# A spectral block and a GeGLU block on one core: last filter groups in other banks, squares a slice later, two norms on Pool, the table load behind the first x pieces

## The chip, the cores and the metric

The kernel runs on one core of a Trainium2 chip. The metric is the device time of one execution in microseconds (us). The kernel before takes 511.15 us (median of 4 runs, 511.12 to 511.28). A profile is one execution recorded by the hardware; its span is about 2 us shorter than the device time (509.6 us for the profiled run of the kernel before, which took 511.58 us), as the device time contains what surrounds the span.

Engines: PE multiplies matrices, DVE (VectorE), ACT (ScalarE) and Pool (GpSimd) do the elementwise work, SP here only issues transfers. The program gives each engine its own list of instructions, in an order stated by hand, and makes it wait on semaphores for the others. Matmuls write their results to PSUM, of which the program uses eight banks, numbered 0 to 7, and DVE or ACT evict them (copy them out) to SBUF. Idle matmuls are matmuls whose results are never used.

## The reference

```python
def reference(A_x, A_w_r, A_w_i, B_x, B_w_gate, B_w_up, B_w_down):   # x: 1 x 2048 x 576 bf16
    x = A_x
    # irfft2(rfft2(layernorm(x)) * (w_r + i w_i)), over the 2048 and the 576
    h = x + _A_ref(_layernorm(x, axis=-1), A_w_r, A_w_i)
    # (gelu(n @ w_gate) * (n @ w_up)) @ w_down, hidden size 4608
    return h + _B_ref(_layernorm(h, axis=-1), B_w_gate, B_w_up, B_w_down)
```

The first half is a two-dimensional Fourier filter, computed with matmuls against cosine tables. The second half is a gated feed-forward block, about 427 of the 510 us.

## The kernel before

The program runs through five stages.

1. Start, up to about 22 us. x arrives in five pieces (rows of tiles 0-1, 2-3, 4-7, 8-11, 12-15). Mean and variance of each 128-row tile come from DVE (`bn_stats`) or, for tiles 3, 7, 11 and 13, from ACT. A table ATB is scaled by each tile's reciprocal deviation (ATS), PE multiplies, ACT and DVE evict to U.
2. The d transform, 22 to 53 us: sixteen filter groups, each through D (PE, sums on DVE into CUS), B (PE, evicted by ACT into YS), products with the filter (T1, T2 on DVE), their difference and sum (ZS, on Pool), and V (PE, evicted by ACT).
3. The tail: the last three groups' V.
4. The inverse: sixteen slices, `st_I` then `st_N`, residual added on DVE. The first four tiles are also normed and transposed on PE here for the next stage.
5. Gate/up and down products, from 82.5 us to the end.

The parts that matter, with cuts marked by `...`:

```python
# start: loads
for i, (c0, c1) in enumerate(((0, 2), (2, 4), (4, 8), (8, 12), (12, 16))):
    P.dma(SP, XO[:, c0:c1, 0:D], xv[:, c0:c1, :], f"x{i}", ...)
P.dma(ACT, ATB[...], dram["ATAB"][:, :], "atb", w=["ATB"])        # 512 KB
...
# start: order of the statistics (each call adds instructions to one or two engines)
ln1_act(3); idle_mm(18); ln1_tile(0); ln1_tile(1); ln1_var(0); ln1_sqrt(0)
ln1_act(7); ln1_tile(2); ln1_scale(0, POOL); ln1_var(1); ln1_sqrt(1); ...
ln1_sqrt(3); ln1_tile(12); ln1_scale(3, POOL); ln1_var(4); ...

# d transform, group i (st_B, its last lines): Pool but for the last two groups
ze = POOL if i < NG - 2 else DVE
P.op(ze, ... ZS[:, z3, 0, 0:KW] = T1[..., 0, :] - T1[..., 1, :] ...)
P.op(ze, ... ZS[:, z3, 1, 0:KW] = T2[..., 0, :] + T2[..., 1, :] ...)

def st_V(i):                                    # all groups in banks 6 and 7
    for c in range(3):
        for zp in range(2): P.op(PE, ... matmul(bank(6 + c // 2, ...), ZS[...], VT[...]) ...)
    P.op(ACT, ... V[:, :, :, g, :] <- banks 6, 7 ...)

for i in range(NG + 3):                         # NG = 16
    if i < NG: st_D(i)
    if 1 <= i <= NG: st_B(i - 1)
    if i > NG: idle_ft(5, 2 * (i - NG - 1))     # idle matmuls
    if i >= 3: st_V(i - 3)
idle_ft(5, 4)

# inverse
def st_N(c):
    ... four matmuls ...; DVE: x[c] += result, with its row sum
    if c < 4: square(c, ...)                    # ACT: row sum of squares of x[c]
TURN = (7, 9, 11, 13)                           # slices after which a tile is transposed
for c in range(NT):
    if c == 6: ln2_b(0)                         # ACT: sqrt
    st_I(c)                                     # 6 matmuls, ACT evicts into GS
    if c >= 1: st_N(c - 1)
    if c == 5: ln2_a(0)                         # DVE: three small ops
    if c == 6: ln2_c(0)                         # DVE: reciprocal
    if c in (6, 8, 10, 12): norm((c - 6) // 2)  # DVE
    if c in TURN: turn_pe(TURN.index(c))        # PE transpose, ACT evicts
```

Of the kernel before, what the change touches and what calls it, by code (L numbers as in the profile page):

```python
# [4 lines left out]
BF16 = mybir.dt.bfloat16  # L5
F32 = mybir.dt.float32
ACTF = mybir.ActivationFunctionType
ALU = mybir.AluOpType

S, D, K2 = 2048, 576, 289  # L10
# [5 lines left out]
NG = 16  # L16
# [279 lines left out]
def _build(nc, A_x, A_w_r, A_w_i, B_w_gate, B_w_up, B_w_down, out):  # L296
    P = Prog(nc)
# [6 lines left out]
    sb = SbufMap(nc, base, top)  # L304
    XO = sb.alloc("XO", [128, NT, D], BF16)
    WGU = sb.alloc("WGU", [128, 9, FF], BF16)
    HN = sb.alloc("HN", [128, 2, 640], BF16)
    IDT = sb.alloc("IDT", [128, 128], BF16)
    ST1 = sb.alloc("ST1", [128, NT, 2, 6], F32)
    MV1 = sb.alloc("MV1", [128, NT, 2], F32)  # L310
# [40 lines left out]
    T1 = sb.alloc("T1", [128, 2, 2, KW], BF16)  # L351
    T2 = sb.alloc("T2", [128, 2, 2, KW], BF16)
    ZS = sb.alloc("ZS", [128, 3, 2, ZW], BF16)
    SQ = sb.alloc("SQ", [128, 2, D], BF16)
    sb.off = v_off
    AT = sb.alloc("AT", [128, 36, 512], BF16)
    HT1 = sb.alloc("HT1", [128, 5, 512], BF16)
# [16 lines left out]
    ov = out[0].rearrange("(p c) d -> p c d", c=NT)  # L374
    for i, (c0, c1) in enumerate(((0, 2), (2, 4), (4, 8), (8, 12), (12, 16))):
        P.dma(SP, XO[:, c0:c1, 0:D], xv[:, c0:c1, :], f"x{i}", w=[("X", c) for c in range(c0, c1)])
    P.dma(ACT, ATB[:, :, :].rearrange("p a b -> p (a b)"), dram["ATAB"][:, :], "atb", w=["ATB"])
    P.dma(SP, FT[:, :, :, :].rearrange("p a b c -> p (a b c)"), dram["FTAB"][:, :], "ft", w=["FT"])
    P.dma(SP, BT[:, :, :, :].rearrange("p a b c -> p (a b c)"), dram["BTAB"][:, :], "bt", w=["BT"])
    P.dma(SP, VT[:, :, :, :].rearrange("p a b c -> p (a b c)"), dram["VTAB"][:, :], "vt", w=["VT"])  # L380
# [57 lines left out]
    def ln1_scale(i, eng):  # L438
        c0, c1 = GROUPS[i]
        P.op(DVE, lambda v, c0=c0, c1=c1: v.reciprocal(RS1[:, c0:c1], RS1[:, c0:c1]), r=[("SD1", i)], w=[("RS1", i)])  # L440
        if eng == POOL:
            P.op(POOL, lambda g, c0=c0, c1=c1: g.tensor_tensor(ATS[:, c0:c1, :], ATB[:, c0:c1, :],
                                                               RS1[:, c0:c1].unsqueeze(2).to_broadcast([128, c1 - c0, 128]), op=ALU.mult),
                 r=[("RS1", i), "ATB"], w=[("ATS", c) for c in range(c0, c1)])
        else:
            for c in range(c0, c1):
                P.op(DVE, lambda v, c=c: v.tensor_scalar(ATS[:, c, :], ATB[:, c, :], RS1[:, c:c + 1], None, op0=ALU.mult),
                     r=[("RS1", i), "ATB"], w=[("ATS", c)])
# [43 lines left out]
    ln1_sqrt(0)  # L492
    ln1_act(7)
    ln1_tile(2)
    ln1_scale(0, POOL)
    ln1_var(1)
    ln1_sqrt(1)
    ln1_tile(4)
# [14 lines left out]
    ln1_var(3)  # L513
    ln1_sqrt(3)
    ln1_tile(12)
    ln1_scale(3, POOL)
    ln1_var(4)
    idle_mm(5)
    a_group(2, A5, lambda: ln1_sqrt(4), 2)
    ln1_tile(14)  # L520
# [30 lines left out]
    def st_B(i):  # L551
        g = GORD[i]
        sl = i % 2
        sp_ = 1 if g == 0 else 0

        for b, tabs in ((4, (0, 1, 3)), (5, (1, 2, 0))):
            for m, (tb, pl, q0, q1) in enumerate(((tabs[0], 0, 0, K2), (tabs[1], 1, 0, HK), (tabs[2], 1, HK, K2))):
                P.op(PE, lambda t, b=b, tb=tb, pl=pl, q0=q0, q1=q1, m=m, sl=sl, sp_=sp_: t.matmul(  # L558
                    bank(b, 0, 128, q0, q1), BT[:, sp_, tb, :], CUS[:, sl, pl, q0:q1], start=(m == 0), stop=(m == 2)),
                    r=[("CU", sl), ("SU", sl), "BT"], w=[("PS", b)])  # L560
        P.op(ACT, lambda a, sl=sl: a.activation(YS[:, sl, :, 0:K2], banks(4, 2, K2), ACTF.Copy), r=[("PS", 4), ("PS", 5)], w=[("Y", sl)])  # L561
        wk = wkeys[0 if 1 <= g < 9 else 1] + ["Wz", "Yz", "Zz"]
        P.op(DVE, lambda v, g=g, sl=sl: v.tensor_tensor(T1[:, sl, :, :], YS[:, sl, :, :], WS[:, g, :, :], op=ALU.mult), r=[("Y", sl)] + wk, w=[("T1", sl)])
        P.op(DVE, lambda v, g=g, sl=sl: v.tensor_tensor(T2[:, sl, :, :], YS[:, sl, :, :], WS[:, g, 1::-1, :], op=ALU.mult), r=[("Y", sl)] + wk, w=[("T2", sl)])  # L564
        z3 = i % 3
        ze = POOL if i < NG - 2 else DVE
        P.op(ze, lambda v, sl=sl, z3=z3: v.tensor_tensor(ZS[:, z3, 0, 0:KW], T1[:, sl, 0, :], T1[:, sl, 1, :], op=ALU.subtract), r=[("T1", sl)], w=[("Z", z3, 0)])
        P.op(ze, lambda v, sl=sl, z3=z3: v.tensor_tensor(ZS[:, z3, 1, 0:KW], T2[:, sl, 0, :], T2[:, sl, 1, :], op=ALU.add), r=[("T2", sl)], w=[("Z", z3, 1)])  # L568

    def st_V(i):  # L570
        g = GORD[i]
        sl = i % 3
        sp_ = 1 if g == 0 else 0
        for c in range(3):
            b, o = 6 + c // 2, 256 * (c % 2)
            for zp in range(2):
                P.op(PE, lambda t, b=b, o=o, c=c, zp=zp, sl=sl, sp_=sp_: t.matmul(bank(b, 0, 128, o, o + 256), ZS[:, sl, zp, 128 * c:128 * c + 128],  # L577
                                                                                  VT[:, sp_, zp, :], start=(zp == 0), stop=(zp == 1)),
                     r=[("Z", sl, 0), ("Z", sl, 1), "Zz", "VT"], w=[("PS", b)])
        P.op(ACT, lambda a, g=g: a.activation(V[:, :, :, g, :], PS[:, 6 * 512:6 * 512 + 768].rearrange("p (k n e) -> p k n e", k=6, n=16), ACTF.Copy),  # L580
             r=[("PS", 6), ("PS", 7), "Vfree"], w=[("V", g)])

    def idle_ft(n, b):
        for _ in range(n):
# [4 lines left out]
    for i in range(NG + 3):  # L589
        if i < NG:  # L590
            st_D(i)
        if 1 <= i <= NG:
            st_B(i - 1)
        if i > NG:
            idle_ft(5, 2 * (i - NG - 1))
        if i >= 3:
            st_V(i - 3)
    idle_ft(5, 4)


    wdv = B_w_down[:, :].rearrange("(c p) d -> p c d", p=128)
# [8 lines left out]
    P.alias(["FT", "BT", "VT"], [("HT", 0, i, k) for i in range(4) for k in range(5)])  # L610


    vkeys = [("V", g) for g in range(NG)]


    TURN = (7, 9, 11, 13)

    def islot(c):
        return (c + sum(c > t for t in TURN)) % 2
# [16 lines left out]
    def st_N(c):  # L636
        sl = c % 2
        for h in range(2):
            b = 4 + 2 * sl + h
            for i in range(2):  # L640
                rhs = GS[:, sl, i, 288:0:-1] if h else GS[:, sl, i, 0:288]
                P.op(PE, lambda t, b=b, h=h, i=i, c=c, rhs=rhs: t.matmul(bank(b, 0, 128, 0, 288), IT[:, h * i, c, :], rhs, start=(i == 0), stop=(i == 1)),  # L642
                     r=[("G", sl), "IT"], w=[("PS", b)])
        x2 = XO[:, c, 0:D].rearrange("p (a b) -> p a b", a=2)
        P.op(DVE, lambda v, x2=x2, c=c, sl=sl: v.scalar_tensor_tensor(x2, banks(4 + 2 * sl, 2, 288), 1.0, x2, op0=ALU.mult, op1=ALU.add,  # L645
                                                               accum_out=SB2[:, 0, c:c + 1]),
             r=[("PS", 4 + 2 * sl), ("PS", 5 + 2 * sl)], w=[("X", c), ("S0", c)])
        if c < 4:
            square(c, SQ[:, sl, :], ("SQ", sl))


    def ln2_a(q):
# [11 lines left out]
        c0, c1 = ((0, 4), (4, 16))[q]  # L664
        P.op(DVE, lambda v, c0=c0, c1=c1: v.reciprocal(RS2[:, c0:c1], RS2[:, c0:c1]), r=[("SD2", q)], w=[("RS2", q)])

    def norm(c):
        hs = c % 2
        q = min(c // 4, 1)
        for i, (o0, o1, x0, x1) in enumerate(((0, D, 0, D), (D, 640, 512, D))):  # L670
            P.op(DVE, lambda v, c=c, hs=hs, o0=o0, o1=o1, x0=x0, x1=x1: v.tensor_scalar(HN[:, hs, o0:o1], XO[:, c, x0:x1], TM[:, 1, c:c + 1],
                                                                                        RS2[:, c:c + 1], op0=ALU.subtract, op1=ALU.mult),
                 r=[("X", c), ("MN", q), ("RS2", q)], w=[("HN", hs, i)])

    def turn_dma(c):
        hs = c % 2
        q = c // 4
        HT = HTS[q % 2]
        for k in range(5):
            P.dma(SP, HT[:, k, 128 * (c % 4):128 * (c % 4) + 128], HN[:, hs, 128 * k:128 * k + 128], f"tr{c}",  # L680
                  r=[("HN", hs, 0), ("HN", hs, 1)], w=[("HT", q % 2, c % 4, k)], transpose=True)

    def turn_pe(c):
        hs = c % 2
        t0, t1 = 128 * c, 128 * c + 128
        b0 = 2 * ((TURN[c] + 1 + c) % 2)
        for k in range(5):
            b, o = b0 + k // 4, 128 * (k % 4)
            P.op(PE, lambda t, b=b, o=o, k=k, hs=hs: t.matmul(bank(b, 0, 128, o, o + 128), HN[:, hs, 128 * k:128 * k + 128], IDT[:, :], start=True, stop=True),  # L689
                 r=[("HN", hs, 0), ("HN", hs, 1), "IDT"], w=[("PS", b)])  # L690
        P.op(ACT, lambda a, t0=t0, t1=t1, b0=b0: a.activation(HT0[:, 0:5, t0:t1], PS[:, b0 * 512:b0 * 512 + 640].rearrange("p (k e) -> p k e", k=5), ACTF.Copy),
             r=[("PS", b0), ("PS", b0 + 1)], w=[("HT", 0, c, 0)])

    for c in range(NT):
        if c == 6:
            ln2_b(0)
        st_I(c)
        if c >= 1:
            st_N(c - 1)
        if c == 5:  # L700
            ln2_a(0)
        if c == 6:
            ln2_c(0)
        if c in (6, 8, 10, 12):
            norm((c - 6) // 2)
        if c in TURN:
            turn_pe(TURN.index(c))


    fdead = vkeys + ["DT", "IT", ("G", 0), ("G", 1), ("Y", 0), ("Y", 1), "Yz", "Zz", ("SQ", 0), ("SQ", 1)]  # L710
    fdead += [(n_, a) for n_ in ("T1", "T2", "E") for a in range(2)] + [("Z", a, b_) for a in range(3) for b_ in range(2)]
    fnew = ([("AT", f) for f in range(36)] + [("GL", 0), ("GL", 1)] + [("HT", 1, i, k) for i in range(4) for k in range(5)])

# [100 lines left out]
```

## Time and profile before

The head of the page of the kernel before, with the span and the busy time of each engine (share of the span, number of instructions):

```profile
span 509.6 us, 10004 instructions
...
PE 497.7 (98%) x4337; PEld 289.6 (57%) x4337; DVE 183.1 (36%) x375; ACT 158.6 (31%) x296; POOL 42.1 (8%) x60
```

PE is busy nearly always, but this counts idle matmuls too, so it doesn't tell what a change of the first 82 us is worth. The chain of waits does: it goes back from the last instruction to whatever released each step. Its columns are the start, the duration and the work.

```profile
1.67 6.46 DMA XO<-in_A_x_dram
...
85.17 70.04 PE PS L731 x648
155.21 35.39 PE PS L752 x288
```

From 85 us on the chain is PE alone, in four pairs of stretches of 70.0 and 35.4 us. Ahead of that the chain goes through many engines, and it begins with a wait for x. Only this first part can be shortened by the change. It is best cut at four moments, which I read from the timeline:

| kernel before | us |
|---|---|
| ACT begins tile 7, the first use of x piece 2 | 8.15 |
| first D matmul | 22.05 |
| first matmul of the inverse | 59.16 |
| first gate/up matmul | 82.46 |
| end of the span | 509.6 |

In the timeline the columns are start, duration, engine, line of the program, operation, output and inputs, count, and in brackets how long the engine idled before it and what released it. A count, with its duration, stops where the window asked for ends, so the same group can show x12 in one view and x5 in another. `SPq` and `ACTq` are issues of transfers. The start, before:

```profile
0.74 0.37 ACTq L206 DMA_DIRECT2D ATB<-c_atab  x1
...
0.75 2.57 SPq L206 DMA_DIRECT2D XO<-in_A_x_dram  x5
...
6.17 0.68 ACT L411 ACTIVATE JNK<-XO 128x576 bf16<-128x576 bf16 x1 [3.53 <-DMA XO<-in_A_x_dram]
...
8.15 0.68 ACT L411 ACTIVATE JNK<-XO 128x576 bf16<-128x576 bf16 x1 [0.36 <-DMA XO<-in_A_x_dram]
...
15.85 0.98 DVE L430 SCALAR_TENSOR_TENSOR MV_54<-SA,TM 128x1 f32<-128x1 f32 x1
...
22.05 1.66 PE L541 MATMUL PS<-FT,U 128*128 128x290 bf16 x12 [0.35 <-DVE U L474]
```

The table and the five pieces of x are issued at the same moment, on two queues. ACT waits for x piece 2 until 8.15 us. One 128x1 statistics op on DVE (line 430) takes 0.98 us; the same line takes 0.16 us elsewhere in this trace.

The tail of the d transform, before:

```profile
51.82 0.82 POOL L567 TENSOR_TENSOR ZS<-T_80 128x290 bf16<-128x290 bf16 x1 [0.40 <-DVE T_80 L563]
...
52.79 0.96 POOL L568 TENSOR_TENSOR ZS<-T_81 128x290 bf16<-128x290 bf16 x1
...
53.89 0.81 PE L577 MATMUL PS<-VT,ZS 128*128 128x256 bf16 x6 [0.22 <-POOL ZS L568]
...
55.61 0.83 PE L577 MATMUL PS<-VT,ZS 128*128 128x256 bf16 x6 [0.28 <-ACT V L580]
...
56.48 0.81 ACT L580 ACTIVATE V<-PS 128x768 bf16<-128x768 f32 x1 [0.92 <-PE PS L577]
...
57.34 0.83 PE L577 MATMUL PS<-VT,ZS 128*128 128x256 bf16 x6 [0.28 <-ACT V L580]
...
59.16 1.66 PE L627 MATMUL PS<-DT,V 128*128 128x289 bf16 x12 [0.37 <-ACT V L580]
```

Two Pool ops make group 13's ZS. Then V of groups 13, 14 and 15 and their evictions alternate, since they share banks 6 and 7, and the inverse starts behind the last eviction.

A piece of the inverse, before:

```profile
62.40 0.68 ACT L633 ACTIVATE SQ<-XO 128x576 bf16<-128x576 bf16 x1 [0.89 <-DVE XO L645]
...
63.08 0.63 ACT L629 ACTIVATE GS<-PS 128x578 bf16<-128x578 f32 x1
...
63.77 0.67 PE L642 MATMUL PS<-GS,IT 128*128 128x288 bf16 x4 [0.22 <-ACT GS L629]
...
69.59 0.67 PE L642 MATMUL PS<-GS,IT 128*128 128x288 bf16 x4 [0.29 <-ACT GS L629]
```

On ACT a square waits for DVE's new x, the next eviction (GS) queues behind the square, and PE waits for that eviction: at 63.77, at 66.65 in the same way, and at 69.59 (there behind the sqrt).

### The profile page before, as it was taken

Reading aid. Unit: us, or ns where it says so; the run is one execution under the profiler, and the core shown is the slowest. Engines: PE = TensorE matmul, PEld = TensorE weight load, DVE = VectorE, ACT = ScalarE, POOL = GpSimd, SP = SyncE. Lnnn points to the kernel's source line nnn. Section 1 sums busy time; section 2 is a strip of 40 time slices with the busy share of each in tenths; the row PEclk is TensorE's granted clock in tenths of the full one; section 3 lists DMA queues with packets and bytes.
Section 4 is the critical chain, followed back from the end, with each engine's and each line's share of the span. In section 5 each row is a group of like instructions: output and inputs, shape, how many; then the busy total and the mean of one; then the engine's idle time right before and its main releaser. Section 6 shows DMA issues by size and latency. Waiting matters only on the chain.

```text
span 509.6 us, 10004 instructions
## 1 busy us (share of the span) xinstructions
PE 497.7 (98%) x4337; PEld 289.6 (57%) x4337; DVE 183.1 (36%) x375; ACT 158.6 (31%) x296; POOL 42.1 (8%) x60
## 2 busy tenths in 40 slices
PE   6899899999999999999999999999999999999997
PEld 2578565444447774444467754444577644444776
DVE  5899464334431113433321124333311133333111
ACT  6778676664230003232310022333200132323000
POOL 3278910000000000000000000000000000000000
PEclk9999999999999999999999999999999999999999
DMA  8679798000100000110000001100000000000000
GB/s 320 134 259 309 224 343 277 1 1 17 27 12 9 16 19 17 23 22 1 1 7 18 13 15 24 23 7 1 1 17 19 13 1 1 1 1 1 13 18 19
DMA packets 25660, 28.64 MB, mean 56 GB/s; under 512 B 11408, under 2 KB 19600, under 8 KB 25488
## 3 DMA queue, kind: packets, MB, share of 16 engines
q1 hardware_dynamic: 22896, 16.86, 11.4%
q0 software_dynamic: 2576, 10.62, 6.2%
q8 instruction: 34, 0.56, 0.5%
q10 hardware_dynamic: 144, 0.52, 0.3%
q14 instruction: 10, 0.08, 0.1%
HBM read 23.66 MB, written 2.36 MB: 51 GB/s over the span
## 4 chain that ended last, share of the span: by engine, by line
PE 90%; DVE 4%; ACT 3%; DMA 1%; POOL 1%; issue 1%; SPq 0%; DVEq 0%; POOLq 0%
PE PS L731 55%; PE PS L752 28%; PE PS L577 2%; PE PS L541 2%; DMA XO<-in_A_x_dram 1%; PE PS L642 1%; PE PS L558 1%; PE PS L627 1%; DVE XO L645 1%; DVE U L474 1%; ACT U L476 1%; ACT V L580 0%; ACT JNK L411 0%; POOL ZS L568 0%; PE PS L689 0%
## 5 line engine op out<-in xcount | busy, mean ns | idle before, releaser
L743 ACT ACTIVATE GL<-PS 128x512 bf16<-128x512 f32 x144 | 85.9, 597 | 289.9 <-PE PS L731 289.9
L744 DVE TENSOR_TENSOR AT<-GL,PS 128x512 bf16<-128x512 bf16 x144 | 98.9, 688 | 174.2 <-PE PS L731 172.5
L731 PE MATMUL PS<-HT_69,WGU 64*128 64x512 bf16 x1296 | 144.4, 376 | 0.0
L731 PE MATMUL PS<-HT_85,WGU 64*128 64x512 bf16 x1296 | 144.4, 376 | 0.0
L752 PE MATMUL PS<-WD,AT 128*128 128x288 bf16 x1152 | 141.8, 286 | 0.0
L752 PEld LDWEIGHTS PS<-WD,AT 128*128 128x128 bf16 x1152 | 112.4, 98 | 29.9 <-issue 1.7
L731 PEld LDWEIGHTS PS<-HT_85,WGU 64*128 64x128 bf16 x1296 | 64.3, 94 | 78.1 <-issue 0.5
L731 PEld LDWEIGHTS PS<-HT_69,WGU 64*128 64x128 bf16 x1296 | 64.5, 94 | 76.8 <-issue 0.7
L755 DVE TENSOR_TENSOR OS<-PS,XO 128x288 bf16<-128x288 f32 x32 | 14.6, 458 | 126.0 <-PE PS L752 126.0
L645 DVE SCALAR_TENSOR_TENSOR XO<-PS,XO 128x576 bf16<-128x576 f32 x16 | 12.1, 757 | 15.4 <-PE PS L642 15.4
L627 PE MATMUL PS<-DT,V 128*128 128x289 bf16 x96 | 14.4, 287 | 0.4 <-ACT V L580 0.4
L541 PE MATMUL PS<-FT,U 128*128 128x290 bf16 x96 | 14.4, 287 | 0.3 <-DVE U L474 0.3
L577 PE MATMUL PS<-VT,ZS 128*128 128x256 bf16 x96 | 13.1, 272 | 1.0 <-ACT V L580 0.6
L580 ACT ACTIVATE V<-PS 128x768 bf16<-128x768 f32 x16 | 13.0, 810 | 3.3 <-PE PS L577 2.8
L568 POOL TENSOR_TENSOR ZS<-T_81 128x290 bf16<-128x290 bf16 x14 | 12.3, 878 | 2.4 <-DVE CUS L548 0.5
L564 DVE TENSOR_TENSOR T_81<-YS,WS 128x580 bf16<-128x580 bf16 x16 | 12.5, 778 | 0.0
L558 PE MATMUL PS<-CUS,BT 128*128 128x289 bf16 (+2 forms) x96 | 10.7, 246 | 1.1 <-DVE CUS L548 0.8
L561 ACT ACTIVATE YS<-PS 128x578 bf16<-128x578 f32 x16 | 10.5, 655 | 4.3 <-PE PS L558 2.6
L629 ACT ACTIVATE GS<-PS 128x578 bf16<-128x578 f32 x16 | 10.3, 647 | 3.7 <-PE PS L627 3.4
L418 DVE BATCH_NORM_STATS2 ST_53<-XO 128x6 f32<-128x288 bf16 x24 | 9.3, 441 | 5.6 <-DMA XO<-in_A_x_dram 5.6
L642 PE MATMUL PS<-GS,IT 128*128 128x288 bf16 x64 | 10.5, 286 | 0.8 <-ACT GS L629 0.7
L452 PE MATMUL PS<-ZD 128*128 128x512 bf16 x30 | 10.0, 485 | 1.3 <-POOL ZD L370 1.3
(60 smaller groups left out, 184.2 us busy)
## 6 DMA issues: line engine op xcount, KB each, us to landing
WD<-in_B_w_down_dram POOLq DMA_DIRECT2D x9, 576.0 KB, 19.7
WGU<-in_B_w_up_dram SPq DMA_DIRECT2D x4, 1152.0 KB, 12.8
WGU<-in_B_w_gate_dram POOLq DMA_DIRECT2D x4, 1152.0 KB, 10.1
out_dram<-OS SPq DMA_DIRECT2D x32, 72.0 KB, 1.6
XO<-in_A_x_dram SPq DMA_DIRECT2D x3, 576.0 KB, 7.4
IT<-c_itab SPq DMA_DIRECT2D x1, 1024.0 KB, 5.6
HT_85<-HN SPq DMA_TRANSPOSE x40, 2.4
XO<-in_A_x_dram SPq DMA_DIRECT2D x2, 288.0 KB, 4.9
```

The lines of the kernel that those rows point to most:

```text
L541: P.op(PE, lambda t, b=b, o=o, dt=dt, us=us, g=g: t.matmul(bank(b, 0, 128, 0, 2 * HK), U[:, us, g, :, :], FT[:, o, dt, :], start=(dt == 0) ...
L558: P.op(PE, lambda t, b=b, tb=tb, pl=pl, q0=q0, q1=q1, m=m, sl=sl, sp_=sp_: t.matmul(bank(b, 0, 128, q0, q1), BT[:, sp_, tb, :], CUS[:, sl, ...
L577: P.op(PE, lambda t, b=b, o=o, c=c, zp=zp, sl=sl, sp_=sp_: t.matmul(bank(b, 0, 128, o, o + 256), ZS[:, sl, zp, 128 * c:128 * c + 128], VT[ ...
L580: P.op(ACT, lambda a, g=g: a.activation(V[:, :, :, g, :], PS[:, 6 * 512:6 * 512 + 768].rearrange("p (k n e) -> p k n e", k=6, n=16), ACTF. ...
L627: P.op(PE, lambda t, b=b, h=h, i=i, kt=kt, c=c: t.matmul(bank(b, 0, 128, 0, K2), V[:, kt, c, :, :], DT[:, 3 * h + i, 0:K2], start=(i == 0) ...
L642: P.op(PE, lambda t, b=b, h=h, i=i, c=c, rhs=rhs: t.matmul(bank(b, 0, 128, 0, 288), IT[:, h * i, c, :], rhs, start=(i == 0), stop=(i == 1) ...
L645: P.op(DVE, lambda v, x2=x2, c=c, sl=sl: v.scalar_tensor_tensor(x2, banks(4 + 2 * sl, 2, 288), 1.0, x2, op0=ALU.mult, op1=ALU.add, accum_o ...
L731: op = P.op(PE, lambda t, h0=h0, kt=kt, wt=wt, f=f, b=b, HT=HT, s=(half == 0 and j in (0, 5)), e=(half == 1 and j in (3, 8)): t.matmul(ban ...
L743: P.op(ACT, lambda a, s2=s2, b0=b0: a.activation(GL[:, s2, :], bank(b0), ACTF.Gelu_apprx_tanh), r=[("PS", b0)], w=[("GL", s2)])
L744: P.op(DVE, lambda v, s2=s2, b0=b0, f=f: v.tensor_tensor(AT[:, f, :], GL[:, s2, :], bank(b0 + 1), op=ALU.mult), r=[("GL", s2), ("PS", b0 + ...
L752: P.op(PE, lambda t, b=b, h=h, f=f, p=p: t.matmul(bank(b, 0, 128, 0, 288), AT[:, f, 128 * p:128 * p + 128], WD[:, f, 288 * h:288 * h + 288 ...
L755: P.op(DVE, lambda v, b=b, h=h, p=p, c=c: v.tensor_tensor(OS[:, p % 2, 288 * h:288 * h + 288], bank(b, 0, 128, 0, 288), XO[:, c, 288 * h:2 ...
```

## The change

Its intent: (a) the first x pieces should not share the transfer engines with the 512 KB table; (b) the last groups of the d transform should overlap matmuls and evictions and stay off slow Pool; (c) in the inverse, squares should run a slice later so that ACT doesn't wait, and the norms should be ready well before the transposes, with half of them on Pool. The diff, cut to its core:

```diff
-    HN = sb.alloc("HN", [128, 2, 640], BF16)
+    HN = sb.alloc("HN", [128, 4, 640], BF16)
...
     for i, (c0, c1) in enumerate(((0, 2), (2, 4), (4, 8), (8, 12), (12, 16))):
         P.dma(SP, XO[:, c0:c1, 0:D], xv[:, c0:c1, :], f"x{i}", w=...)
-    P.dma(ACT, ATB[...], dram["ATAB"][:, :], "atb", w=["ATB"])
+        if i == 1:
+            P.dma(SP, ATB[...], dram["ATAB"][:, :], "atb", w=["ATB"])
...
-    ln1_scale(0, POOL)
+    ln1_scale(0, DVE)
...
+    ln1_var(4)
     ln1_scale(3, POOL)
-    ln1_var(4)
...
-        ze = POOL if i < NG - 2 else DVE
+        ze = POOL if i < NG - 3 else DVE
...
+        b0 = {NG - 2: 0, NG - 1: 2}.get(i, 6)      # st_V: first bank
-        P.op(ACT, ... V[:, :, :, g, :] <- banks 6, 7 ...)
+        if i < NG - 1:
+            P.op(ACT, ... V[:, :, :, g, :] <- banks b0, b0 + 1 ...)
+        else:
+            P.op(DVE, ... V[:, 0:4, :, g, :] <- bank b0 ...)
+            P.op(ACT, ... V[:, 4:6, :, g, :] <- bank b0 + 1 ...)
...
-        if i > NG:
-            idle_ft(5, 2 * (i - NG - 1))
+        if i == NG + 2:
+            idle_ft(5, 4)
...
-    idle_ft(5, 4)
+    idle_ft(4, 4)
...
-    TURN = (7, 9, 11, 13)
+    TURN = (10, 11, 12, 13)
...                                                 # st_N
-        if c < 4:
-            square(c, SQ[:, sl, :], ("SQ", sl))
...                                                 # loop over slices
-        if c == 6:
-            ln2_b(0)
         st_I(c)
         if c >= 1:
             st_N(c - 1)
-        if c == 5:
+        if 2 <= c < 6:
+            square(c - 2, OS[:, c % 2, :], ("OS", c % 2, 0))
+        if c == 6:
             ln2_a(0)
-        if c == 6:
+            ln2_b(0)
+        if c == 7:
             ln2_c(0)
-        if c in (6, 8, 10, 12):
-            norm((c - 6) // 2)
+            norm(0, DVE)
+            norm(1, POOL)
+        if c == 8:
+            norm(2, DVE)
+            norm(3, POOL)
         if c in TURN:
             turn_pe(TURN.index(c))
```

More of the change, by code (lines that the diff above doesn't have):

```diff
@@ L353, in _build @@
     ZS = sb.alloc("ZS", [128, 3, 2, ZW], BF16)
-    SQ = sb.alloc("SQ", [128, 2, D], BF16)
     sb.off = v_off
@@ L376, in _build @@
         P.dma(SP, XO[:, c0:c1, 0:D], xv[:, c0:c1, :], f"x{i}", w=[("X", c) for c in range(c0, c1)])
-    P.dma(ACT, ATB[:, :, :].rearrange("p a b -> p (a b)"), dram["ATAB"][:, :], "atb", w=["ATB"])
+        if i == 1:
+            P.dma(SP, ATB[:, :, :].rearrange("p a b -> p (a b)"), dram["ATAB"][:, :], "atb", w=["ATB"])
     P.dma(SP, FT[:, :, :, :].rearrange("p a b c -> p (a b c)"), dram["FTAB"][:, :], "ft", w=["FT"])
@@ L573, in st_V @@
         sp_ = 1 if g == 0 else 0
+        b0 = {NG - 2: 0, NG - 1: 2}.get(i, 6)
         for c in range(3):
-            b, o = 6 + c // 2, 256 * (c % 2)
+            b, o = b0 + c // 2, 256 * (c % 2)
             for zp in range(2):
@@ L579, in st_V @@
                      r=[("Z", sl, 0), ("Z", sl, 1), "Zz", "VT"], w=[("PS", b)])
-        P.op(ACT, lambda a, g=g: a.activation(V[:, :, :, g, :], PS[:, 6 * 512:6 * 512 + 768].rearrange("p (k n e) -> p k n e", k=6, n=16), ACTF.Copy),
-             r=[("PS", 6), ("PS", 7), "Vfree"], w=[("V", g)])
+        src = PS[:, b0 * 512:b0 * 512 + 768].rearrange("p (k n e) -> p k n e", k=6, n=16)
+        rk = [("PS", b0), ("PS", b0 + 1), "Vfree"]
+        if i < NG - 1:
+            P.op(ACT, lambda a, g=g, src=src: a.activation(V[:, :, :, g, :], src, ACTF.Copy), r=rk, w=[("V", g, 0)])
+        else:
+            P.op(DVE, lambda v, g=g, src=src: v.tensor_copy(V[:, 0:4, :, g, :], src[:, 0:4, :, :]), r=rk[0:1] + rk[2:], w=[("V", g, 0)])
+            P.op(ACT, lambda a, g=g, src=src: a.activation(V[:, 4:6, :, g, :], src[:, 4:6, :, :], ACTF.Copy), r=rk[1:], w=[("V", g, 1)])
     def idle_ft(n, b):
@@ L610, in _build @@
     P.alias(["FT", "BT", "VT"], [("HT", 0, i, k) for i in range(4) for k in range(5)])
-    vkeys = [("V", g) for g in range(NG)]
-    TURN = (7, 9, 11, 13)
+    vkeys = [("V", g, 0) for g in range(NG)] + [("V", GORD[NG - 1], 1)]
+    TURN = (10, 11, 12, 13)
     def islot(c):
@@ L665, in ln2_c, with norm @@
         P.op(DVE, lambda v, c0=c0, c1=c1: v.reciprocal(RS2[:, c0:c1], RS2[:, c0:c1]), r=[("SD2", q)], w=[("RS2", q)])
-    def norm(c):
-        hs = c % 2
+    def norm(c, eng=DVE):
+        hs = c % 4
         q = min(c // 4, 1)
         for i, (o0, o1, x0, x1) in enumerate(((0, D, 0, D), (D, 640, 512, D))):
-            P.op(DVE, lambda v, c=c, hs=hs, o0=o0, o1=o1, x0=x0, x1=x1: v.tensor_scalar(HN[:, hs, o0:o1], XO[:, c, x0:x1], TM[:, 1, c:c + 1],
+            P.op(eng, lambda v, c=c, hs=hs, o0=o0, o1=o1, x0=x0, x1=x1: v.tensor_scalar(HN[:, hs, o0:o1], XO[:, c, x0:x1], TM[:, 1, c:c + 1],
                                                                                         RS2[:, c:c + 1], op0=ALU.subtract, op1=ALU.mult),
@@ L675, in turn_dma @@
     def turn_dma(c):
-        hs = c % 2
+        hs = c % 4
         q = c // 4
@@ L683, in turn_pe @@
     def turn_pe(c):
-        hs = c % 2
+        hs = c % 4
         t0, t1 = 128 * c, 128 * c + 128
@@ L699, in _build @@
             st_N(c - 1)
-        if c == 5:
+        if 2 <= c < 6:
+            square(c - 2, OS[:, c % 2, :], ("OS", c % 2, 0))
+        if c == 6:
             ln2_a(0)
-        if c == 6:
+            ln2_b(0)
+        if c == 7:
             ln2_c(0)
-        if c in (6, 8, 10, 12):
-            norm((c - 6) // 2)
+            norm(0, DVE)
[3 more added lines that the diff above has]
+            norm(3, POOL)
         if c in TURN:
             turn_pe(TURN.index(c))
-    fdead = vkeys + ["DT", "IT", ("G", 0), ("G", 1), ("Y", 0), ("Y", 1), "Yz", "Zz", ("SQ", 0), ("SQ", 1)]
+    fdead = vkeys + ["DT", "IT", ("G", 0), ("G", 1), ("Y", 0), ("Y", 1), "Yz", "Zz"]
     fdead += [(n_, a) for n_ in ("T1", "T2", "E") for a in range(2)] + [("Z", a, b_) for a in range(3) for b_ in range(2)]
```

## The prediction

> **What bounds it.** By the busy table PE is busy 98% of 509.6 us. By the chain of waits, everything from 82.53 us on is PE (four 70.04 us gate/up stretches, four 35.4 us down stretches); the change leaves that alone. Only the first 82.5 us can move.
>
> **Tail of the d transform** (timeline 50 to 59 us). Before, group 13's subtract and add run on Pool, 51.82-53.76, twice as long as on DVE (0.83+0.97 against 0.30+0.30). Then three V groups run serially through banks 6 and 7: matmuls 0.83, eviction 0.82, three times, 53.89-59.02; the inverse starts at 59.16. The change gives group 13 to DVE and separate banks to the last two groups, so evictions overlap matmuls, and splits the last eviction (DVE two thirds, about 0.62 by half of the two 128x512 casts' 1.24; ACT one third, about 0.35). It adds 0.44 us on DVE ahead of the last CUS pair, so the last B matmuls move from 53.00 to about 53.4, YS ends about 54.8, group 15's Z is ready about 56.05, its V matmuls end about 56.95, the eviction about 57.4. Inverse starts about 57.5: **-1.6 us**. The Trainium skill ("SBUF — State Buffer", section "SBUF: two separate sides") says VectorE and GpSimd share an exclusively locked port pair; the trace agrees (T2 0.45 us alone, 0.93 under a Pool op), so DVE also loses one such wait.
>
> **Inverse** (59.16 to 82.53, 23.37 us). Pure PE period is 1.245 us a slice. The timeline shows PE waits of about 0.4, 0.4 (the square waits for DVE's X, and the next GS eviction queues behind it), 0.47 (sqrt before GS 7) and four of 0.17-0.19 at the turns (transpose waits for its DVE norm). With squares a slice later ACT runs GS+square dense at 1.24 us, just PE's period; norms are ready three slices before the turns. A new or remaining wait of 0.35-0.4 stays at slice 7, where sqrt waits in ACT's queue for three small DVE ops behind the sixth residual add. Two Pool norms (estimate 1.4 us each from Pool's 0.61 at 256 and 1.04 at 512 elements) have slack. **-1.4 us**.
>
> **Start.** x pieces 0 and 1 no longer share the engines with the 512 KB table (the skill, "DMA: Bandwidth & Descriptors", "Queues, rings and completion order": engines take turns between queues), so they land about 1 us earlier and the table about 1 us later. But from x piece 2's landing (8.13) ACT is dense to about 17 us, and the bytes up to that landing are the same, so this gives nothing (0 to +0.3). var(4) before scale(3) takes a 0.98 us statistics op, stuck behind Pool's scale, out of DVE's chain; sqrt(4) stays limited by ACT evictions, so about **-0.3**.
>
> Sum -3.3, less 0.1 for the start: **507.9 us**, eight in ten 506.8 to 509.4. Chances: faster by over 2% 0.005, within 2% 0.99, slower 0.005.
>
> **What would show it.** D's first matmul at 21.7-22.1 (before 22.05). Inverse's first matmul at about 57.3 (before 59.16), its DVE and ACT evictions side by side. Inverse to first gate/up matmul about 21.9 (before 23.37), with no wait before N(2), N(4) or the turns, one of about 0.4 before N(7). After that the stretches are unchanged to 0.1 us.
>
> **What would make it wrong.** x piece 2 landing later than 8.4 with the table ahead of it in the same ring; ACT at 1.24 us against PE at 1.245 losing step; a Pool norm much longer than 1.4 us, or locking DVE's residual adds out (slack about 1.1 us); the strided DVE copy slower than 0.62; PE's clock dropping in a new gap; Pool's earlier weight issues crowding the table loads.

## The result, and the profile after

The changed kernel takes 508.70 us (median of 4 runs, 508.59 to 509.02), against 511.15 us. The ratio of the fast runs is 0.9953, with a 95% interval of 0.9935 to 0.997. Ratios here are the mean time of one kernel's fast runs over the mean of the other's fast runs of the same rounds, so they are not quite the ratios of the medians I quote. The record marks each run as fast or slow by its time and clock; all runs in this document are fast ones. The prediction was 507.9 us with a range of 506.8 to 509.4: the range holds, and the saving is 2.45 us where about 3.2 were forecast.

```profile
span 506.9 us, 9999 instructions
...
PE 496.6 (98%) x4331; PEld 290.1 (57%) x4331; DVE 182.4 (36%) x376; ACT 157.6 (31%) x296; POOL 46.1 (9%) x61
```

| | before | after | difference | predicted |
|---|---|---|---|---|
| ACT begins tile 7 | 8.15 | 8.88 | +0.73 | 0 to +0.3 |
| from there to the first D matmul | 13.90 | 13.59 | -0.31 | -0.3 |
| first D matmul to the inverse | 37.11 | 35.44 | -1.67 | -1.6 |
| inverse to first gate/up matmul | 23.30 | 21.89 | -1.41 | -1.4 |
| first gate/up matmul to the end | 427.14 | 427.10 | -0.04 | 0 |

Every row is a difference of two starts in the timeline. Four of five terms came out as forecast; the first one did not. The start, after:

```profile
0.74 0.87 SPq L206 DMA_DIRECT2D XO<-in_A_x_dram  x2
...
1.66 0.42 SPq L206 DMA_DIRECT2D ATB<-c_atab  x1
...
4.51 0.68 ACT L411 ACTIVATE JNK<-XO 128x576 bf16<-128x576 bf16 x1 [2.27 <-DMA XO<-in_A_x_dram]
...
7.43 0.41 DVE L447 TENSOR_SCALAR ATS<-ATB,RS_56 128x128 bf16<-128x128 bf16 x2 [1.10 <-DMA ATB<-c_atab]
...
8.88 0.68 ACT L411 ACTIVATE JNK<-XO 128x576 bf16<-128x576 bf16 x1 [2.74 <-DMA XO<-in_A_x_dram]
...
16.56 0.16 DVE L430 SCALAR_TENSOR_TENSOR MV_54<-SA,TM 128x1 f32<-128x1 f32 x1
...
22.47 0.78 PE L541 MATMUL PS<-FT,U 128*128 128x290 bf16 x5 [0.35 <-DVE U L474]
```

The first two pieces do land early: ACT begins tile 3 at 4.51 and not at 6.17 us. But the table, third on the same queue, is not there until 7.43 us (DVE waits 1.10 us for it), and x piece 2 behind it comes at 8.88. The statistics op of line 430 is back at 0.16 us.

The tail, after:

```profile
52.30 0.30 DVE L567 TENSOR_TENSOR ZS<-T_80 128x290 bf16<-128x290 bf16 x1
...
52.74 0.45 DVE L547 TENSOR_TENSOR CUS<-ES,PS 128x290 bf16<-128x290 f32 x1
...
53.70 0.67 PE L558 MATMUL PS<-CUS,BT 128*128 128x289 bf16 x6 [0.68 <-DVE CUS L548]
...
54.21 1.47 PE L579 MATMUL PS<-VT,ZS 128*128 128x256 bf16 x12
...
56.43 0.83 PE L579 MATMUL PS<-VT,ZS 128*128 128x256 bf16 x6
...
57.07 0.69 DVE L587 CAST V<-PS 128x512 bf16<-128x512 f32 x1 [0.71 <-PE PS L579]
...
57.29 0.38 ACT L588 ACTIVATE V<-PS 128x256 bf16<-128x256 f32 x1 [0.72 <-PE PS L579]
...
57.91 1.66 PE L634 MATMUL PS<-DT,V 128*128 128x289 bf16 x12 [0.16 <-DVE V L587]
```

V of group 14 no longer waits for an eviction (the twelve matmuls at 54.21 are groups 13 and 14 in one run), the last eviction runs on DVE and ACT side by side, and the inverse starts 1.48 us after the last V began (57.91 less 56.43), where it took 1.82 us before (59.16 less 57.34). The first two lines show the price: group 13's two ops (the second begins at 52.52) stand on DVE just ahead of the last CUS pair.

The inverse, after (ACT, ACT, PE):

```profile
62.34 0.65 ACT L636 ACTIVATE GS<-PS 128x578 bf16<-128x578 f32 x1
...
62.89 0.68 ACT L640 ACTIVATE OS<-XO 128x576 bf16<-128x576 bf16 x1
...
68.80 0.67 PE L649 MATMUL PS<-GS,IT 128*128 128x288 bf16 x4 [0.29 <-ACT GS L636]
```

GS and square now follow each other on ACT with no wait, and PE's waits are gone but for one, at 68.80, where the sqrt stands in front of GS. The two norms on Pool, from the groups of instructions by shape (busy us, mean ns, idle before):

```profile
L676 POOL TENSOR_SCALAR HN<-XO,TM,RS_59 128x576 bf16<-128x576 bf16 x2 | 4.8, 2404 | 2.9 <-DVE RS_59 L670 2.8
L676 POOL TENSOR_SCALAR HN<-XO,TM,RS_59 128x64 bf16<-128x64 bf16 x2 | 1.2, 578 | 0.2
```

A norm on Pool takes 2.40 + 0.58 us, not the estimated 1.4. It ends in time here: PE shows no wait before a transpose, so this costs nothing.

### The profile page after: what moved, and what is told of

The parts are those of the page before. It is cut to its first block, busy times and chain, and to the rows that moved or that the text cites. A ratio compares the mean times of both kernels' runs of the same rounds, so it can differ in the third digit from the quotient of the medians.

```text
span 506.9 us, 9999 instructions
## 1 busy us (share of the span) xinstructions
PE 496.6 (98%) x4331; PEld 290.1 (57%) x4331; DVE 182.4 (36%) x376; ACT 157.6 (31%) x296; POOL 46.1 (9%) x61
## 4 chain that ended last, share of the span: by engine, by line
PE 90%; DVE 4%; ACT 2%; DMA 1%; issue 1%; POOL 0%; SPq 0%; DVEq 0%; POOLq 0%
PE PS L740 56%; PE PS L761 28%; PE PS L634 2%; PE PS L649 2%; DMA XO<-in_A_x_dram 1%; PE PS L541 1%; PE PS L579 1%; DVE T_80 L563 1%; ACT U L476 1%; DVE CUS L547 1%; PE PS L558 1%; DVE CUS L548 1%; DVE T_81 L564 1%; DVE U L474 1%; ACT JNK L411 0%
## 5 line engine op out<-in xcount | busy, mean ns | idle before, releaser
L541 PEld LDWEIGHTS PS<-FT,U 128*128 128x128 bf16 x96 | 9.2, 98 | 2.9 <-issue 0.8
```

What stands on the lines that cost most here:

```text
L541: P.op(PE, lambda t, b=b, o=o, dt=dt, us=us, g=g: t.matmul(bank(b, 0, 128, 0, 2 * HK), U[:, us, g, :, :], FT[:, o, dt, :], start=(dt == 0) ...
```

## The experiments

Theory: the parts of the change add up, three of them give what the prediction said, and the table's new place alone makes x piece 2 late. Rival: the start was late by chance or for another reason, or the parts eat into each other. Twelve kernels were run; each gave a correct result. They ran in three rounds, on different chips, with the kernel before among them: its medians were 511.21, 511.24 and 511.21 us. The changed kernel was not run again, so a difference from its 508.70 us is one between rounds.

### The table move alone

```diff
 kernel before
-    P.dma(ACT, ATB...)
+        if i == 1: P.dma(SP, ATB...)      # third on the x queue
```

> The kernel before with only the table load moved onto the x queue behind the first two x pieces. Theory: this move alone is what made the start of the changed kernel later: x piece 2 (tiles 4-7) lands about 0.7 us later (8.13 to about 8.86) and, as ACT is dense from there, the whole kernel is 0.6 to 0.8 us slower (about 511.9). Rival (the prediction): the same bytes precede that landing, so it lands within 0.2 us of 8.13 and the time stays at 511.1 to 511.4.

Measured: 511.94 us (511.23 to 512.45), ratio 1.0014 (1.0001 to 1.0026). ACT begins tile 7 at 8.71 us. The move costs 0.73 us by the medians, though these runs scatter by 1.2 us; the theory's size holds, the prediction's "the same bytes" does not.

### The table back on ACT's queue

```diff
 changed kernel
-        if i == 1: P.dma(SP, ATB...)
+    P.dma(ACT, ATB...)
```

> The changed kernel with only the table load put back on ACT's queue at the start. Theory: x piece 2 lands at about 8.1 again, D's first matmul is at about 21.75, and the kernel gains 0.7 us on the changed one (about 508.0), beating it. Rival: the start is late for another reason (group 0's scale on DVE, or chance between runs) and the time stays at 508.7.

Measured: 507.68 us (507.58 to 507.90), ratio to before 0.9932 (0.9919 to 0.9944). That is 1.02 us below the changed kernel's 508.70. ACT begins tile 7 at 7.70 us, at once after tile 3, so x piece 2 was there by then; the first D matmul is at 21.27:

```profile
6.16 0.68 ACT L410 ACTIVATE JNK<-XO 128x576 bf16<-128x576 bf16 x1 [3.53 <-DMA XO<-in_A_x_dram]
...
7.70 0.67 ACT L410 ACTIVATE JNK<-XO 128x576 bf16<-128x576 bf16 x1
```

That the undo gives 1.02 us and the move 0.73 is within the scatter: by the mean spans of all runs the move costs 0.92 us (510.08 less 509.16) and the undo gains 0.86 (506.60 less 505.74). The profiled run of the kernel before was a late one: in this kernel and the next two, which load alike, tile 7 begins at 7.70, 7.78 and 7.85 us, and not at 8.15. In these three the chain of waits begins with x piece 1 (issued at 1.20 us, landing 4.94 to 5.09 us later), and x piece 2 holds nothing up.

### The tail alone

```diff
 kernel before
+ group 13 on DVE, banks 0 and 2 for groups 14 and 15, split last eviction, moved idle matmuls
```

> The kernel before with only the tail of the d transform changed (group 13 on DVE, separate banks for the last two groups, split last eviction, idle matmuls moved). Theory: gain of 1.67 us as read between D's first matmul and the inverse's first in the two traces, about 509.5. Rival: the two stages share something (weight loads, buffers), so the terms don't add and it is below 1.3 us.

Measured: 509.65 us (509.51 to 509.79), 1.56 us below before. From the first D matmul to the inverse it takes 35.64 us (before 37.11). The theory holds, with 0.1 to 0.2 us less than expected.

### The inverse alone

```diff
 kernel before
+ squares a slice later, sqrt behind slice 6, two norms on Pool, turns at 10 to 13, four HN buffers
```

> The kernel before with only the inverse's part changed (squares a slice later, sqrt after the residual of slice 5, two norms on Pool, turns at slices 10 to 13). Theory: gain of 1.41 us, about 509.7; the three parts and the table (+0.73), less 0.31 for the reordered statistics, then add up to the whole -2.5. Rival: less, since Pool norms of 3.1 us collide with the WD issues that start later relative to it.

Measured: 509.86 us (509.72 to 509.99), 1.35 us below before. From the inverse to gate/up it takes 21.89 us, just as in the changed kernel. With the reorder's 0.31 us (below), the parts sum to -1.56 - 1.35 - 0.31 = -3.22 us, and the table brings back 0.73 (alone) to 1.02 (undone): -2.49 to -2.20 us, against the measured -2.45. They add.

### Two x pieces merged

```diff
 changed kernel
-    ((0, 2), (2, 4), (4, 8), (8, 12), (12, 16)), table behind the second
+    ((0, 4), (4, 8), (8, 12), (12, 16)),         table behind the first
```

> The changed kernel with x pieces 0 and 1 merged into one load, the table still right behind them in the same queue: x piece 2 is then issued third and not fourth, at about 1.67 us as in the kernel before, not 2.13. Theory A (the extra 0.46 us of issue ahead of x piece 2 delays it): it lands at about 8.4 and the kernel is about 0.4 us faster than the changed one. Theory B (one queue alone moves the same bytes more slowly than two in the first microseconds): it lands at 8.7 to 8.9 and the time stays within 0.15 us of 508.7.

Measured: 507.69 us (507.47 to 507.82), 1.01 us below the changed kernel; tile 7 begins at 7.57 us. Neither theory gives this size. B falls: x piece 2 lands 5.88 us after its issue at 1.66 us; with the table on ACT's queue the middle one of the five x loads, which is this piece, takes 5.9 us from its issue. So one queue alone brought the same bytes as early as two. A has the direction, but 0.46 us of issue cannot give 1.31 us (8.88 less 7.57).

The stretches of the trace show the rest. The last column is what the transfer engines moved, in GB/s, the one before it their busy share (which can read a little over 1). The kernel before, from 4.5 to 6.5 us:

```profile
core 0: us, PE busy (x) PEld busy (x) DVE busy (x) ACT busy (x) POOL busy (x), PEclk, DMA share, GB/s
...
4.50:6.50 2.00, 2.00 (x10) 0.88 (x9) 0.91 (x3) 0.33 (x1) 0.00 (x0) 1.00 1.04 394
```

The changed kernel, then the table move alone, in the same stretch:

```profile
4.50:6.50 2.00, 2.00 (x8) 0.77 (x7) 1.79 (x7) 1.63 (x5) 0.00 (x0) 1.00 0.87 220
```

```profile
4.50:6.50 2.00, 2.00 (x10) 0.85 (x9) 1.81 (x8) 1.63 (x5) 0.00 (x0) 1.00 0.91 253
```

With the pieces merged:

```profile
4.50:6.50 2.00, 2.00 (x6) 0.71 (x5) 1.59 (x6) 1.44 (x4) 0.00 (x0) 1.00 1.03 418
```

With the table third behind two short pieces, throughput falls to 220 and 253 GB/s for two microseconds (269 to 292 in the three other kernels with the table third, where tile 7 begins at 8.35 to 8.85 us). The engines' busy share stays at 0.87 and 0.91, so this is not simply a lack of work for them. With merged pieces, the same table on the same queue, issued 0.46 us earlier, passes at 418 GB/s. At 418 instead of 220 GB/s for 2 us some 0.40 MB more are moved, which at 418 GB/s is worth 0.95 us: the larger part of the 1.31 us.

### Group 13 back on Pool

```diff
 changed kernel
-        ze = POOL if i < NG - 3 else DVE
+        ze = POOL if i < NG - 2 else DVE
```

> The changed kernel with group 13's subtract and add back on Pool, the new banks and the split eviction kept. Theory: on DVE they stand ahead of the last CUS pair (0.44 us on the chain) while B's matmuls of group 15 stand ahead of V's of group 13 on PE anyway, so this gains 0.3 to 0.45 us on the changed kernel (about 508.3). Rival (the intent of the change): Pool's slower pair (1.9 us) makes V of group 13 late, and it loses 0.3 us or more.

Measured: 508.68 us (508.04 to 509.00), not to be told from 508.70 with this spread. The trace is clearer, as it allows taking the late and scattered start off: from the first D matmul to the inverse it takes 35.24 us, 0.20 less than in the changed kernel. Later traces agree: the two versions below with group 13 on Pool read 35.19 us, and six further traces with it on DVE and the changed inverse 35.44 to 35.49. The tail of this run (Pool, PE, PE; its first D matmul was at 21.94, so 0.53 us are to be added when comparing with the changed kernel):

```profile
52.57 0.67 POOL L568 TENSOR_TENSOR ZS<-T 128x290 bf16<-128x290 bf16 x1
...
52.78 0.67 PE L558 MATMUL PS<-CUS,BT 128*128 128x289 bf16 x6 [0.24 <-DVE CUS L548]
...
57.18 0.79 PE L634 MATMUL PS<-DT,V 128*128 128x289 bf16 x5 [0.16 <-DVE V L587]
```

PE runs B of group 15 (52.78) ahead of V of group 13 anyway, and Pool's ops are done when it gets there. So this one edit of the change costs time rather than saves it. The gain is 0.2 and not 0.3 to 0.45 us: DVE's next product again waits for Pool's op, 0.98 us where the changed kernel has 0.45 at that place.

### The sqrt one slice later

```diff
 changed kernel
         if c == 6:
             ln2_a(0)
-            ln2_b(0)
         if c == 7:
-            ln2_c(0); norm(0, DVE); norm(1, POOL)
+            ln2_b(0)
         if c == 8:
-            norm(2, DVE); norm(3, POOL)
+            ln2_c(0); norm(0, DVE); norm(1, POOL)
+        if c == 9:
+            norm(2, DVE); norm(3, POOL)
```

> The changed kernel with sqrt one slice later (behind GS 7 in ACT's queue) and the norms one slice later. Theory: the one PE wait left in the inverse, 0.60 us before N(7), goes, gain 0.4 us (about 508.3). Rival: the Pool norms (3.1 us each) end too late for the turns at slices 11 or 13, a new wait eats it.

Measured: 508.82 us (508.52 to 509.70), no gain in the times. In the trace the inverse takes 21.64 us, 0.25 less than 21.89 (21.63 in the two versions below that share the edit, 21.89 in all other traces with the changed inverse): the wait before N(7) is gone, and a new one of 0.2 us, at 74.28 us, stands before the second transpose, whose norm on Pool ends only then. So the rival is right in part. The times don't show the gain, as they scatter by 1.2 us; the profiled run, the slowest, lost 1.04 us elsewhere: from tile 7 to the first D matmul it took 14.63 us, not 13.59. A stretch of this run (the third column from the right is PE's granted clock):

```profile
16.00:18.00 2.00, 1.67 (x11) 1.08 (x11) 1.50 (x9) 2.00 (x6) 1.04 (x1) 0.50 0.88 187
```

The same stretch of the changed kernel:

```profile
16.00:18.00 2.00, 1.61 (x15) 0.69 (x12) 1.50 (x9) 2.00 (x7) 1.04 (x1) 1.00 0.91 198
```

PE had half its clock from 14 to 18 us here and 0.58 from 18 to 20 us, in the very stage in which its matmuls feed the evictions: ACT waits 0.68 us for them at 19.37 us and DVE 0.91 us at 19.80.

### The statistics op behind Pool's scale again

```diff
 changed kernel
-    ln1_var(4)
     ln1_scale(3, POOL)
+    ln1_var(4)
```

> The changed kernel with var(4) behind scale(3) again. Theory: the small statistics op waits out Pool's 1.04 us scale again (0.98 instead of 0.16 us) in DVE's chain, and D starts 0.3 us later: 509.0. Rival: with the whole start later, ACT's evictions hide it and the time stays within 0.1 us of 508.7.

Measured: 509.17 us (508.34 to 510.33). The times are too scattered to settle 0.3 us. The trace settles it: line 430 takes 0.98 us again, and from tile 7 to the first D matmul it takes 13.90 us against 13.59.

```profile
16.55 0.98 DVE L430 SCALAR_TENSOR_TENSOR MV<-SA,TM 128x1 f32<-128x1 f32 x1
```

The reorder is worth 0.31 us. Other traces agree: four more with the old order take 13.89 to 13.94 us, four more with the new one 13.57 to 13.59 (left out are the sqrt experiment, above, and the three kernels below with the table behind x piece 2, where other waits enter the stretch and it takes 13.67 to 15.09). This kernel and the table move alone differ up to the first D matmul only in group 0's scale, on DVE here and on Pool there, and take 13.90 and 13.89 us, so that edit is worth nothing in this stretch.

### The table behind x piece 2

```diff
 changed kernel
-        if i == 1: P.dma(SP, ATB...)
+        if i == 2: P.dma(SP, ATB...)
```

> The changed kernel with the table fourth on the x queue, behind x piece 2 and not ahead of it. Question: in the four traces with the table third, DMA throughput falls from about 400 to 120-260 GB/s between 4.5 and 6.5 us, when the third load of the queue begins. Theory P (the third load after two short ones starts before the queue is ready for it, whatever it loads): the fall stays, x piece 2 lands at 7 us or later. Theory T (it is the table's own read there): x piece 2 lands at about 6.1 to 6.3 with no fall ahead of it. Either way the table lands later than 7.4 and group 0 then waits for it; time 507.5 to 508.8.

Measured: 508.07 us (507.63 to 508.98). x piece 2 was there when ACT wanted it, at 5.96 us, and the stretch from 4.5 to 6.5 us reads:

```profile
4.50:6.50 2.00, 2.00 (x6) 0.69 (x5) 1.75 (x8) 2.00 (x6) 0.00 (x0) 1.00 1.01 366
```

With x piece 2 third, throughput dips only to 366 GB/s, and x piece 2 came one microsecond before the 7 us that theory P asked for. So theory P, that any third load stumbles, falls. Theory T has the landing right, but the table is not slow in itself: it passed at full rate when it stood second, and it does so third behind two loads of 576 KB (e11 below: issued at 1.67 us, as in the changed kernel, with 418 GB/s from 4.5 to 6.5 us and 425 from 6.5 to 8.5). Here the rate stays at 364 and 373 GB/s from 6.5 to 10 us too. What remains is the combination: the worst stumble is with the table directly behind two short pieces. Why it stumbles there stays open. The table lands at 7.99 us here and then holds up group 0.

### The versions put together

```diff
 changed kernel
+ e10: pieces 0 and 1 merged, group 13 on Pool, sqrt a slice later
+ e11: pieces 0 and 1 merged, table behind x piece 2 (which is then the second load)
+ e12: e11 with group 13 on Pool, sqrt a slice later
```

> The merged load of x pieces 0 and 1, with group 13 back on Pool and sqrt and norms one slice later. Theory: the three gains add to the changed kernel: 1.0 (measured) + 0.2 + 0.25 (as read between D's, the inverse's and the gate/up's first matmuls in the single traces, where the spread of the start hid them in the times): 507.2. Rival: they don't add, no better than 507.6.

Measured: 507.11 us (507.02 to 507.19), 0.58 us below the merged load alone (0.45 expected). Here, with a start that scatters little, the two small gains do show in the time.

> The changed kernel with x pieces 0 and 1 merged and the table behind x piece 2. Theory: x piece 2 lands at about 6.2, ACT runs tile 7 from 6.4, the table lands about 7.5, and ACT's chain starts 0.7 us or more earlier than with the merged load alone: 506.8 to 507.1. Rival: the table becomes the limit (group 0's evictions wait for it) and nothing is gained, 507.5 to 507.8.

Measured: 507.17 us (506.99 to 507.39), 0.52 us below the merged load with the table ahead of x piece 2. Tile 7 begins at 7.13 us; the first piece pair lands at 5.1 us here and what precedes tile 7 on ACT and DVE is the limit, so the gain is less than the expected 0.7.

> The run before this one with group 13 on Pool and sqrt and norms one slice later: 0.45 us below it, about 506.5, if those two gains and the start are independent.

Measured: 506.61 us (506.34 to 506.71), ratio to before 0.9909 (0.9896 to 0.9923): the fastest of all, 2.1 us below the changed kernel and 0.56 us below e11 (0.45 expected). Its first D matmul is at 20.53 us, the inverse at 55.72, gate/up at 77.35, and its span is 504.4 us.

## Why the prediction was right or wrong

- Which part can move: right. From the first gate/up matmul on, 427.14 and 427.10 us.
- The tail: right, -1.67 us in the trace for a forecast of -1.6, -1.56 alone in the times. Forecast and measured pieces agree (DVE's part of the last eviction 0.62 against 0.69 us, ACT's 0.35 against 0.38). What I missed is that one of its edits, group 13 on DVE, is worth +0.2 us, which is a loss; I had written down the 0.44 us it adds and not asked whether anything is gained for it.
- The inverse: right in size and in detail, -1.41 for -1.4 us, with the one wait left before N(7). Pool's norms were mis-sized by a factor of two (1.4 estimated, 2.98 measured), without effect.
- The reorder of the statistics: right, 0.31 for 0.3 us.
- The start as a whole: wrong in sign. The failed step is "the bytes up to that landing are the same, so this gives nothing (0 to +0.3)". The bytes are the same, but the rate at which they come is not: 220 GB/s against 394 from 4.5 to 6.5 us. The move costs 0.73 us alone and 1.02 us when undone. The first D matmul came at 22.47 us, outside the stated 21.7 to 22.1, and "x piece 2 landing later than 8.4 with the table ahead of it in the same ring" was listed among what could go wrong. The Trainium skill ("DMA: Bandwidth & Descriptors", section "Queues, rings and completion order") says that the transfer engines take turns between queues; the early landing of pieces 0 and 1 (tile 3 at 4.51 against 6.17 us) agrees. It didn't follow that the rest would be neutral. The 0.8 us by which the time lies above the forecast is about what this one step cost.
- A second, smaller point: I took 8.15 us from one profiled run as typical. That run was late; three other traces with the same loads have 7.70 to 7.85. So "from x piece 2's landing ACT is dense" described a late run; in the other three it is dense from x piece 1's landing, at 6.16 to 6.31 us.
- Shown and not shown: that the table's place causes the loss is shown by the move alone and by its undoing. That the fall in throughput is the larger part of it rests on the arithmetic above. What makes the transfers slow there is open. Moving group 0's scale from Pool to DVE was not tried on its own, but two experiments that differ there only in it take the same time from tile 7 to the first D matmul (13.90 and 13.89 us).

## What to carry to other kernels

Equal bytes ahead of a transfer do not mean an equal landing time: order and size of the loads on a queue can change the rate (here 220 to 292 against 418 GB/s), so read the landing of the transfer that the chain waits for, and try merged and reordered loads before moving them. When a change has several edits, cut the trace at a few fixed moments and account for each stretch alone; effects of 0.2 us that the times of a scattered start hide are plain there. An op moved to a faster engine still stands ahead of something else in that engine's queue, so ask what it delays.

## What the Trainium skill lacked or had wrong

- "DMA: Bandwidth & Descriptors": nothing on a load's rate depending on the loads ahead of it on its queue. With a 512 KB load third behind two of 288 KB, the five kernels moved 220 to 292 GB/s from 4.5 to 6.5 us; with it behind one of 576 KB, 418; with a 576 KB load of x in that third place, 366.
- "GPSIMD Engine Reference", section "4.1 Engine selection", calls one-input elementwise work on GpSimd roughly line-rate, in a row that compares it with VectorE. The norm (subtract and multiply by per-partition scalars, 128x576 bf16) has one tensor input and took 2.40 us on Pool (2.52 and 2.29) and 0.42 us on DVE, over five times as long.
- "TensorE: Matmul & The Clock Gate", section "Part 1: The HAM clock gate", says that the clock drops to half after at least one idle window, about 3.4 us. Six traces here show the half clock (0.50 to 0.59 in 2 us stretches between 12 and 20 us) after shorter pauses: PE's longest pause between 2 and 20 us is 1.98 to 2.99 us in these six, and at most 1.40 us in the eight without a half clock. No run isolates the pause. The half clock need not cost anything: from tile 7 to the first D matmul the kernel before took 13.90 us with it around 13 us, and the tail alone 13.91 us without it. In the sqrt experiment, at half clock until almost 20 us, the same stretch took 1.04 us longer. The five kernels with the table third had a mean clock of 0.997 or less in 16 of 24 runs, the other eight changed kernels in 2 of 38; the longer pauses of PE there (2.08 to 2.99 us in the five traces) may be why.
